# A mixture's first products in a seven-product form, with the tokens taken in three passes

## The chip, the cores and the metric

One core of a Trainium2 chip runs the whole program. The metric is the device time of one execution in microseconds (us). TensorE is PE in the profile, VectorE is DVE, ScalarE is ACT, GpSimd is POOL and SyncE, whose queue starts most transfers, is SP.

## What is computed

Three stages follow one another. A small attention between x (4 batches, 8 heads, 512 positions, 64 wide) and a state of 32 rows gives N = 2176 tokens of 512 (17 tiles of 128 tokens). A first mixture of eight experts is dense: every token goes through every expert, and the weights P come from eight rounds of row and column normalisation over all tokens. A second mixture sends each token to one expert.

```
# first mixture: x (N, 512), w1 (8, 512, 1024), w2 (8, 1024, 512)
logits = x @ w_gate
P = np.exp(logits - logits.max())
for _ in range(8):
    P /= P.sum(1, keepdims=True) + 1e-09
    P /= P.sum(0, keepdims=True) + 1e-09
    P *= N / E
for e in range(E):
    out += P[:, e:e + 1] * (np.maximum(x @ w1[e], 0.0) @ w2[e])
# second mixture
e_idx = np.argmax(out @ w_gate2, axis=1)
h = np.maximum(x[mask] @ w1[e], 0.0)          # mask: tokens of expert e
out[mask] = gate_w[mask, None] * eom[mask, e, None] * (h @ w2[e])
```

## The kernel before

**Operands in two parts.** A product of fp32 operands is made of three matmuls: each operand is split into a high part (a cast on ACT to the matmul's 32-bit format) and a low part (what the cast left over, by a subtraction on another engine), and high·high, high·low and low·high are accumulated in one PSUM bank.

**Start.** The attention of batch 0 (parts c1 to c5 per group of four heads: transposes, scores, softmax, transposes, read) runs before the first product. c5 writes the tokens into `xhi` and `xlo` (L238, L239), which hold all of x, transposed and split, on the chip. The parts of batches 1 to 3 and the other half of the attention (n1 to n3, lagging) are in a queue, and `pump` takes entries from it between groups of matmuls, at a pace set per stage.

**Units.** The first mixture is 32 units: expert × quarter (256 of 1024 hidden columns). `prep` loads 512 KB of w1 and of w2 for one unit, `prep_split` casts on ACT (L367) and subtracts on POOL (L368). Each unit goes over five chunks of tokens, three of 512, one of 384 and one of 256. `mm1` makes the hidden values: two halves of 128 hidden columns, four blocks of K, three matmuls each (L386 to L388), then relu on ACT (L389) and the low part of the hidden values on DVE (L390). `mm2` makes, for each 128-token tile of the chunk before, two blocks × three matmuls of 512 columns (L402 to L404); DVE multiplies by the gate and accumulates (L413).

**Gates.** `gate_a` and `gate_b` make the logits from the split x, with the weights stationary. `sinkhorn` is a chain: `row` on DVE (L328 to L332), `col` a matmul with ones (L337) and four operations on DVE (L338 to L341). They are in the queue too, and done before unit 4. The first expert's outputs are added up without gates until then.

**The last unit and after.** A table, `AFTER`, places in the last unit what follows the first mixture: per tile `final_a` (store, four transposes L430), `final_b` (logits of the second mixture, L441); per group of tiles `route` (ranks among an expert's tokens, L473 to L534, with small matmuls L493); `sel_a` to `sel_c` choose what the second mixture starts with; `split_first` splits the first expert's weights in eight pieces of 1024 (L628: ACT casts, POOL subtracts). The second mixture then goes over 19 slots of 128 tokens (`m1`, `hT`, `m2s`; products L678 to L680 and L703 to L705).

## Time and profile before

| | |
|---|---|
| median of three runs | 1910.68 us (1909.02 to 1911.96) |
| the profiled execution: its span | 1910.8 us; the profile gives no other time for it |
| PE busy | 1859.2 us, 97%, 9073 matmuls |
| DVE, ACT, POOL busy | 828.5, 391.1, 228.4 us |
| from the first product to unit 4 | 29.95 to 300.80 us |
| units 4 to 30 | 300.80 to 1558.10 us |
| last unit | 1558.10 to 1636.00 us |
| second mixture | 1636.00 to 1910.80 us |

A row of the timeline has the start, the length, the engine, the line of the kernel, the operation, out<-in by the program's names and shapes; in brackets the idle time before it and what ended that. Matmuls overlap one another, so the length of one is longer than the distance to the next start; the cost of one in a row of many is that distance. The granted clock is a share of full speed.

### The profile page before, as it was taken

Reading aid. Unit: us, or ns where it says so; the run is one execution under the profiler, and the core shown is the slowest. Engines: PE = TensorE matmul, PEld = TensorE weight load, DVE = VectorE, ACT = ScalarE, POOL = GpSimd, SP = SyncE. Lnnn points to the kernel's source line nnn. Section 1 sums busy time; section 2 is a strip of 40 time slices with the busy share of each in tenths; the row PEclk is TensorE's granted clock in tenths of the full one; section 3 lists DMA queues with packets and bytes.
Section 4 is the critical chain, followed back from the end, with each engine's and each line's share of the span. In section 5 each row is a group of like instructions: output and inputs, shape, how many; then the busy total and the mean of one; then the engine's idle time right before and its main releaser. Section 6 shows DMA issues by size and latency. Waiting matters only on the chain. (4 is left out here: it accounts for less than half of the span.)

```text
span 1910.8 us, 22103 instructions
## 1 busy us (share of the span) xinstructions
PE 1859.2 (97%) x9073; PEld 1572.1 (82%) x9073; DVE 828.5 (43%) x1416; ACT 391.1 (20%) x626; POOL 228.4 (12%) x136
## 2 busy tenths in 40 slices
PE   6999999999999999999999999999999999799998
PEld 5788778888888888888888888888888888678886
DVE  4653565344444434444344344434344435834332
ACT  3332111111111111111111111111111112235332
POOL 2000101111111111111111111111111100422212
PEclk9899999999999999999999999999999999899999
DMA  3110000000000000000000000000000004234121
...
DMA packets 55284, 77.38 MB, mean 40 GB/s; under 512 B 22336, under 2 KB 38720, under 8 KB 52608
## 3 DMA queue, kind: packets, MB, share of 16 engines
...
## 5 line engine op out<-in xcount | busy, mean ns | idle before, releaser
L390 DVE SCALAR_TENSOR_TENSOR hl<-ph,hh 128x512 fp32r<-128x512 f32 (+2 forms) x320 | 195.7, 612 | 608.9 <-ACT hh L389 608.9
L386 PE MATMUL ph<-xhi,wh 128*128 128x512 f32 (+2 forms) x1280 | 459.5, 359 | 0.0
L388 PE MATMUL ph<-xhi,wl 128*128 128x512 f32 (+2 forms) x1280 | 457.3, 357 | 0.0
L387 PE MATMUL ph<-xlo,wh 128*128 128x512 f32 (+2 forms) x1280 | 457.0, 357 | 0.0
L402 PE MATMUL py<-wh,hh 128*128 128x512 f32 x1088 | 428.9, 394 | 0.0
L403 PE MATMUL py<-wl,hh 128*128 128x512 f32 x1088 | 425.8, 391 | 0.0
L404 PE MATMUL py<-wh,hl 128*128 128x512 f32 x1088 | 425.6, 391 | 0.0
L389 ACT ACTIVATE hh<-ph 128x512 fp32r<-128x512 f32 (+2 forms) x320 | 170.9, 534 | 1207.8 <-PE ph L388 1205.2
L413 DVE SCALAR_TENSOR_TENSOR accA<-py,PG,accA 128x512 f32<-128x512 f32 x348 | 261.4, 751 | 168.1 <-PE py L404 165.0
L368 POOL TENSOR_TENSOR wl<-raw,wh 128x1024 fp32r<-128x1024 f32 x64 | 153.2, 2395 | 1372.4 <-ACT wh L367 1372.4
L386 PEld LDWEIGHTS ph<-xhi,wh 128*128 128x128 f32 x1280 | 241.3, 188 | 32.9 <-ACT xhi L238 1.2
L387 PEld LDWEIGHTS ph<-xlo,wh 128*128 128x128 f32 x1280 | 241.3, 189 | 31.7
L388 PEld LDWEIGHTS ph<-xhi,wl 128*128 128x128 f32 x1280 | 241.1, 188 | 30.2
L402 PEld LDWEIGHTS py<-wh,hh 128*128 128x128 f32 x1088 | 205.4, 189 | 45.5 <-issue 5.4
L404 PEld LDWEIGHTS py<-wh,hl 128*128 128x128 f32 x1088 | 205.1, 188 | 43.5
L403 PEld LDWEIGHTS py<-wl,hh 128*128 128x128 f32 x1088 | 205.3, 189 | 39.9
L413 DVE SCALAR_TENSOR_TENSOR accB<-py,PG,accB 128x512 f32<-128x512 f32 x145 | 108.9, 751 | 68.0 <-PE py L404 66.7
L367 ACT CAST wh<-raw 128x1024 fp32r<-128x1024 f32 x64 | 66.7, 1044 | 5.1 <-DMA raw<-in_moe_w_dram 5.1
...
L685 ACT ACTIVATE hs<-pm 128x512 f32<-128x512 f32 x38 | 38.4, 1110 | 30.7 <-PE pm L680 30.7
L695 ACT CAST hh<-pt 128x512 fp32r<-128x512 f32 x38 | 20.4, 590 | 104.1 <-PE pt L692 104.1
L696 DVE TENSOR_TENSOR hl<-pt,hh 128x512 fp32r<-128x512 f32 x38 | 24.4, 685 | 38.5 <-ACT hh L695 38.5
...
## 6 DMA issues: line engine op xcount, KB each, us to landing
raw<-in_moe_w_dram SPq DMA_DIRECT2D x64, 512.0 KB, 3.5
...
xg<-x1d,gi POOLq DMA_INDIRECT x20, 4.6
out_dram<-y,si POOLq DMA_INDIRECT x19, 3.0
```

Of the source, the lines that this page charges most:

```text
L367: nc.scalar.copy(hi, raw)
L368: nc.gpsimd.tensor_tensor(out=lo, in0=raw, in1=hi.bitcast(F32), op=ALU.subtract)
L386: nc.tensor.matmul(ps[:, :n], whi[:, k, f], xhi[:, k, cols], start=(k == 0), stop=False)
L387: nc.tensor.matmul(ps[:, :n], whi[:, k, f], xlo[:, k, cols], start=False, stop=False)
L388: nc.tensor.matmul(ps[:, :n], wlo[:, k, f], xhi[:, k, cols], start=False, stop=(k == KD - 1))
L389: nc.scalar.activation(out=hh[:, ft, :n], in_=ps[:, :n], func=AF.Relu)
L390: nc.vector.scalar_tensor_tensor(out=hl[:, ft, :n], in0=ps[:, :n], scalar=0.0, in1=hh[:, ft, :n].bitcast(F32), op0=ALU.max, op1=ALU.subtract)
L402: nc.tensor.matmul(ps, hh[:, j, r], whi[:, j, :], start=(j == 0), stop=False)
L403: nc.tensor.matmul(ps, hh[:, j, r], wlo[:, j, :], start=False, stop=False)
L404: nc.tensor.matmul(ps, hl[:, j, r], whi[:, j, :], start=False, stop=(j == 1))
L413: nc.vector.scalar_tensor_tensor(out=a, in0=ps, scalar=PG[:, t, e : e + 1], in1=a, op0=ALU.mult, op1=ALU.add)
L685: nc.scalar.activation(out=ov, in_=ps2[n].rearrange("t (p j) -> t p j", j=NJ), func=AF.Relu)
```

## The change

**Three passes.** The tokens are taken in three passes of 768, 768 and 640 (`PASSES`, whose second number is half a pass). A pass goes over all 32 units, so there are 96 steps, and in each step the unit's w1 and w2 are loaded and split. x is no longer kept split: c5 writes the tokens of the first pass into `xst` and those of the other passes to DRAM (`xtd`), from which `xload` brings them back at unit 14 of the pass before.

**Seven products.** w1's unit (512 × 256) and a pass's x (512 × 768) are each cut in 2 × 2 blocks. `mm1` makes seven products of 256 × 128 by 256 × 384 (or 320) in Winograd's form of Strassen's method, in the order 1, 6, 5, 7, 2, 3, 4, where product 2 is accumulated onto product 1 in its bank. It needs four sums of blocks of w1 (`prep_w1`, on POOL, per step; seven operands are then split), four sums of blocks of x (`xsums`, per pass; seven operands, `xsplit`), one copy on ACT and six combinations on DVE (L486 to L506) of the products. The relu (L474) and the low part (L478) follow from the combined blocks; of the four low parts, three now have a block in SBUF as their input, not PSUM.

**What else moves.** Batches 0 and 1 of the attention run before the first product; batches 2 and 3, the lagging parts and the gates are in the queue for steps 0 to 4, the normalisation for steps 5 to 7. The gates are made from unsplit x, tile by tile, with x stationary. In the first pass the first two experts are added up without gates. `final_a` and `final_b` run at the end of each pass, `route` for the first four tiles at step 33, for the next two groups with `sel_a` to `sel_c` at steps 65 to 67. Half of the first expert's pieces are split before the second mixture starts. Buffers of the second mixture are laid into those of the first.

```diff
+    PASSES = [(0, 384), (768, 384), (1536, 320)]
+    HW = 384
...
+    def gate(ts):
         def f():
-            t0, nt = CHUNKS[c]
-            n = nt * P
-            cols = slice(t0 * P, t0 * P + n)
-            ps = bank(f"psg{c}")
-            for k in range(KD):
-                nc.tensor.matmul(ps[:, :n], wg_sp[:, k, :], xhi[:, k, cols], start=(k == 0), stop=False)
-                nc.tensor.matmul(ps[:, :n], wg_sp[:, k, :], xlo[:, k, cols], start=False, stop=(k == KD - 1))
-            lt = ap2.tile([P, 2, S], F32, tag="xT", name=f"lt{c}")[:, 0, :]
-            nc.scalar.copy(lt[0 : 2 * E, :n], ps[0 : 2 * E, :n])
-            lts[c] = lt
+            ps = bank(f"psg{ts[0]}")
+            for i, t in enumerate(ts):
+                for k in range(KD):
+                    if t < 6:
+                        a = XT1[:, k, t * P : (t + 1) * P]
+                    elif t < NT - 1:
+                        a = xtm[t // R, k // 2][:, k % 2, (t % R) * P : (t % R + 1) * P]
+                    else:
+                        a = xs[:, k, :]
+                    nc.tensor.matmul(ps[:, i * E : (i + 1) * E], a, wg[:, k, :], start=(k == 0), stop=(k == KD - 1))
...
+    PROD = {1: (0, 0), 2: (1, 1), 3: (6, 2), 4: (2, 6), 5: (3, 3), 6: (4, 4), 7: (5, 5)}
...
+    def xsums(p, home):
+        b11, b12, b21, b22, w = xquarters(p)
+        t = [home[:, i * XW : i * XW + w].rearrange("p (k n) -> p k n", k=2) for i in range(4)]
+        e = nc.vector if p == 0 else nc.gpsimd
+        return [
+            lambda: e.tensor_tensor(out=t[0], in0=b12, in1=b11, op=ALU.subtract),
+            lambda: e.tensor_tensor(out=t[1], in0=b22, in1=t[0], op=ALU.subtract),
+            lambda: e.tensor_tensor(out=t[2], in0=b22, in1=b12, op=ALU.subtract),
+            lambda: e.tensor_tensor(out=t[3], in0=t[1], in1=b21, op=ALU.subtract),
+        ], t
+    def xsplit(p, t, order=(0, 4, 3, 5, 1, 2, 6), pool=(3, 1, 6)):
+        b11, b12, b21, b22, w = xquarters(p)
+        of = [b11, b21, b22] + t
+        def one(i):
+            def f():
+                hi = xop(i, 0, w).rearrange("p (k n) -> p k n", k=2)
+                lo = xop(i, 1, w).rearrange("p (k n) -> p k n", k=2)
+                nc.scalar.copy(hi, of[i])
+                e = nc.gpsimd if i in pool else nc.vector
+                e.tensor_tensor(out=lo, in0=of[i], in1=hi.bitcast(F32), op=ALU.subtract)
+            return f
+        return [one(i) for i in order]
...
+        def f0():
+            nc.gpsimd.tensor_tensor(out=sv[0], in0=a21, in1=a22, op=ALU.add)
+            nc.gpsimd.tensor_tensor(out=sv[1], in0=sv[0], in1=a11, op=ALU.subtract)
+            nc.gpsimd.tensor_tensor(out=sv[2], in0=a11, in1=a21, op=ALU.subtract)
+            nc.gpsimd.tensor_tensor(out=sv[3], in0=a12, in1=sv[1], op=ALU.subtract)
+            nc.scalar.copy(wop(s, 0, 0, 2).rearrange("p (k f) -> p k f", k=KD), raw[:, :, 0:P])
+            nc.scalar.copy(wop(s, 0, 2, 1).rearrange("p (k f) -> p k f", k=2), a22)
+        def f1():
+            nc.scalar.copy(wop(s, 0, 3, 4), sst.rearrange("p a c -> p (a c)"))
+            r = "p (k f) -> p k f"
+            nc.gpsimd.tensor_tensor(out=wop(s, 1, 0, 2).rearrange(r, k=KD), in0=raw[:, :, 0:P],
+                                    in1=wop(s, 0, 0, 2).rearrange(r, k=KD).bitcast(F32), op=ALU.subtract)
+            nc.gpsimd.tensor_tensor(out=wop(s, 1, 2, 1).rearrange(r, k=2), in0=a22,
+                                    in1=wop(s, 0, 2, 1).rearrange(r, k=2).bitcast(F32), op=ALU.subtract)
+            nc.gpsimd.tensor_tensor(out=wop(s, 1, 3, 4), in0=sst.rearrange("p a c -> p (a c)"),
+                                    in1=wop(s, 0, 3, 4).bitcast(F32), op=ALU.subtract)
...
+        def prod(i, ps, start=True, stop=True):
+            a, b = PROD[i]
+            for k in range(2):
+                wh, wl = (wop(s, lo, a, 1)[:, k * P : (k + 1) * P] for lo in (0, 1))
+                xh, xl = (xop(b, lo, 2 * h)[:, k * h : (k + 1) * h] for lo in (0, 1))
+                nc.tensor.matmul(ps, wh, xh, start=start and k == 0, stop=False, skip_group_check=True)
+                nc.tensor.matmul(ps, wh, xl, start=False, stop=False, skip_group_check=True)
+                nc.tensor.matmul(ps, wl, xh, start=False, stop=stop and k == 1, skip_group_check=True)
...
+        def relu(c, f, half):
+            nc.scalar.activation(out=hh[:, f, half * h : (half + 1) * h], in_=c, func=AF.Relu)
+        def rest(c, f, half):
+            q = slice(half * h, (half + 1) * h)
+            nc.vector.scalar_tensor_tensor(out=hl[:, f, q], in0=c, scalar=0.0, in1=hh[:, f, q].bitcast(F32),
+                                           op0=ALU.max, op1=ALU.subtract)
+        tt = nc.vector.tensor_tensor
+        new(1)
+        nc.scalar.copy(u2, B_[1])
+        between(0)
+        new(6)
+        tt(out=u2, in0=B_[6], in1=u2, op=ALU.add)
+        between(1)
+        new(5)
+        tt(out=u4, in0=B_[5], in1=u2, op=ALU.add)
+        between(2)
+        new(7)
+        tt(out=u3, in0=B_[7], in1=u2, op=ALU.add)
+        between(3)
+        prod(2, B_[1], start=False)
+        tt(out=c22, in0=B_[5], in1=u3, op=ALU.add)
+        relu(B_[1], 0, 0)
+        relu(c22, 1, 1)
+        between(4)
+        new(3)
+        rest(B_[1], 0, 0)
+        tt(out=u4, in0=B_[3], in1=u4, op=ALU.add)
+        relu(u4, 0, 1)
+        rest(c22, 1, 1)
+        between(5)
+        new(4)
+        tt(out=u3, in0=u3, in1=B_[4], op=ALU.subtract)
+        relu(u3, 1, 0)
+        rest(u4, 0, 1)
+        between(6)
+        rest(u3, 1, 0)
...
+        if p == 0 and e < 2:
+            if e == 1:
+                a = xst[:, t * DM : (t + 1) * DM]
+            if q == 0:
+                nc.vector.tensor_copy(a, ps)
+            else:
+                nc.vector.tensor_tensor(out=a, in0=ps, in1=a, op=ALU.add)
+            return
...
+        def step_mm1(s):
+            h = PASSES[s // NU][1]
+            nxt = prep_w1(s + 1) if s < LAST else [lambda: None] * 2
+            def between(i):
+                if i == 1:
+                    prep_w2(s)
+                if i == 3:
+                    nxt[0]()
+                if i == 5:
+                    nxt[1]()
+                pump(PITCH[h])
+            mm1(s, between)
+        def step_mm2(s, hooks={}):
+            for t in tiles_of(s // NU):
+                mm2(s, t)
+                if todo:
+                    todo.pop(0)()
+                pump(1.36)
...
+        queue += [gate(range(0, 4)), gate(range(4, 6)), gate(range(6, 8))]
+        for g in range(G):
+            load_x(2, g)
+        load_state(2)
+        load_state(3)
+        queue += window(2) + window(3)
+        (a0, a1, a2), (b0, b1, b2) = lag[2, 0], lag[2, 1]
+        queue += [a0, b0, a1, b1, seq(a2, lambda: load_x(3, 0)), seq(b2, lambda: load_x(3, 1))]
+        (a0, a1, a2), (b0, b1, b2) = lag[3, 0], lag[3, 1]
+        queue += [a0, b0, a1, b1, a2, b2, seq(gate(range(NT - 1, NT)), states_out)]
+        pace[0] = 66.0 / len(queue)
+        queue += [close_reads] + sinkhorn()
...
+            if p < 2 and u == 14:
+                xload(p + 1)
+            if p < 2 and u == 24:
+                sums, T0 = xsums(p + 1, home[0])
+                queue += sums
+                pace[0] = 4.0
+            if s == NU + 1:
+                queue += list(Rq[0])
+                pace[0] = 3.0
+            if s == 2 * NU + 1:
+                queue += [Rq[1][0], seq(Rq[1][1], sel_a), Rq[1][2], Rq[2][0], sel_b, sel_c, Rq[2][1], load_first, first_rows, Rq[2][2]]
+                pace[0] = 4.0
+            step_mm1(s)
+            if u < NU - 1:
+                if u > 0:
+                    step_mm2(s - 1)
+                continue
+            flush()
+            ts = list(tiles_of(p))
+            if p < 2:
+                todo += xsplit(p + 1, T0)
+                step_mm2(s - 1)
+                hooks = {ts[i]: [A[ts[i - 1]]] + ([Bq[ts[i - 2]]] if i > 1 else []) for i in range(1, 6)}
+                step_mm2(s, hooks)
+                while todo:
+                    todo.pop(0)()
+                queue += [seq(A[ts[5]], Bq[ts[4]]), Bq[ts[5]]]
+                pace[0] = 2.0
+            else:
+                load_first_raw(0, 0)
+                for i in (2, 3, 0, 1):
+                    todo.append(lambda i=i: split_piece(SETS[0], i, 1024, nc.gpsimd))
+                todo.append(lambda: load_first_raw(1, 1))
+                step_mm2(s - 1)
+                step_mm2(s, {13: [A[12]], 14: [A[13], Bq[12]], 15: [A[14], Bq[13]], 16: [Bq[14], A[15], lambda: xT(0)]})
+        for i in range(4, 8):
+            split_piece(SETS[0], i, 1024, nc.gpsimd)
```

On POOL, before, two splits stand per unit (`wl_0` is w1's low part, `wl_1` w2's; a unit has five chunks):

```order
L368 TENSOR_TENSOR wl_1_1707<-raw_1_1622,wh_1_1706 128x1024
L368 TENSOR_TENSOR wl_0_2024<-raw_0_1955,wh_0_2023 128x1024
L368 TENSOR_TENSOR wl_1_2113<-raw_1_2021,wh_1_2112 128x1024
L368 TENSOR_TENSOR wl_0_2366<-raw_0_2311,wh_0_2365 128x1024
L368 TENSOR_TENSOR wl_1_2434<-raw_1_2363,wh_1_2433 128x1024
L368 TENSOR_TENSOR wl_0_2674<-raw_0_2621,wh_0_2673 128x1024
```

Now this stands in each of the 96 steps (`sst` holds the sums of w1's blocks, `XR` the split operands, `rawb` the loaded weights, `wl` is w2's low part):

```order
L443 TENSOR_TENSOR wl_4788<-rawb,wh_4787 128x1024
L418 TENSOR_TENSOR sst<-rawb 128x256
L419 TENSOR_TENSOR sst<-sst,rawb 128x256
L420 TENSOR_TENSOR sst<-rawb 128x256
L421 TENSOR_TENSOR sst<-rawb,sst 128x256
L428 TENSOR_TENSOR XR<-rawb,XR 128x512
L430 TENSOR_TENSOR XR<-rawb,XR 128x256
L432 TENSOR_TENSOR XR<-sst,XR 128x1024
L443 TENSOR_TENSOR wl_4915<-rawb,wh_4914 128x1024
```

So a step has eight operations on POOL where a unit of five chunks had two.

On DVE, this is the middle of step 6, in which a row of the normalisation falls (`p_6` are the banks of the step's products, `u` and `c` the combined blocks, `HB` the hidden values, `PG` the gates):

```order
L495 TENSOR_TENSOR c_106<-p_6_1784,u_104 128x384
L328 TENSOR_REDUCE sm_408<-PG 128x17
L329 TENSOR_SCALAR sm_408<-sm_408 128x17
L330 RECIPROCAL sm_409<-sm_408 128x17
L331 TENSOR_TENSOR PG<-PG,sm_409 128x136
L332 TENSOR_REDUCE sm_410<-PG 128x8
L478 SCALAR_TENSOR_TENSOR HB<-p_6_1757,HB 128x384
L501 TENSOR_TENSOR u_105<-p_6_1820,u_105 128x384
L478 SCALAR_TENSOR_TENSOR HB<-c_106,HB 128x384
L506 TENSOR_TENSOR u_104<-u_104,p_6_1836 128x384
L478 SCALAR_TENSOR_TENSOR HB<-u_105,HB 128x384
L338 TENSOR_SCALAR sm_411<-pscol_1846 128x8
```

The operations L328 to L332, which the column matmul waits for, stand between the step's combinations; L478 with `c` and `u` are the low parts from SBUF.

At the end of the first pass, DVE does the accumulations of the last two steps (`py`, L547) with four splits of the next pass's operands (L392) among them:

```order
L547 SCALAR_TENSOR_TENSOR acc<-py_0_5104,PG,acc 128x512
L392 TENSOR_TENSOR XR<-xst,XR 128x768
L547 SCALAR_TENSOR_TENSOR acc<-py_1_5114,PG,acc 128x512
L392 TENSOR_TENSOR XR<-raw_1582,XR 128x768
L547 SCALAR_TENSOR_TENSOR acc<-py_2_5124,PG,acc 128x512
L547 SCALAR_TENSOR_TENSOR acc<-py_3_5134,PG,acc 128x512
L392 TENSOR_TENSOR XR<-raw_1582,XR 128x768
L547 SCALAR_TENSOR_TENSOR acc<-py_4_5144,PG,acc 128x512
L547 SCALAR_TENSOR_TENSOR acc<-py_5_5154,PG,acc 128x512
L392 TENSOR_TENSOR XR<-xst,XR 128x768
L547 SCALAR_TENSOR_TENSOR acc<-py_0_5164,PG,acc 128x512
L547 SCALAR_TENSOR_TENSOR acc<-py_1_5174,PG,acc 128x512
```

The first transposes of the pass's first tile follow on PE after the matmuls of the second `py` of the last step, and need the accumulation of the first, which is the last row but one; before, no split of x stood on DVE beside the tiles' ends.

## Rows read from the trace of the kernel before

**Rows 1.** The page's first part: busy time, share of the span and instructions of each engine.
```profile
PE 1859.2 (97%) x9073; PEld 1572.1 (82%) x9073; DVE 828.5 (43%) x1416; ACT 391.1 (20%) x626; POOL 228.4 (12%) x136
```

**Rows 2.** Engines by stage: start:end, length, busy us and instructions of each engine, granted clock.
```profile
0.00:29.95 29.95, 16.76 (x66) 12.97 (x66) 11.30 (x21) 7.85 (x12) 3.05 (x7) 1.00 0.53 129
29.95:300.80 270.85, 257.48 (x1360) 215.78 (x1359) 146.05 (x325) 66.51 (x133) 23.49 (x24) 0.97 0.09 26
300.80:1558.10 1257.30, 1257.30 (x5995) 1072.41 (x5994) 512.04 (x731) 194.91 (x324) 129.47 (x54) 1.00 0.07 22
1558.10:1636.00 77.90, 74.02 (x454) 64.53 (x452) 41.01 (x157) 19.89 (x38) 5.32 (x4) 1.00 0.40 142
1636.00:1910.80 274.80, 253.65 (x1202) 206.40 (x1202) 118.14 (x184) 101.92 (x121) 67.06 (x48) 0.96 0.27 99
```

**Rows 3.** Timeline of PE: start, length (us), engine, line; first product of units 4 and 31.
```profile
300.80 0.39 PE L386 MATMUL ph<-xhi,wh 128*128 128x512 f32 x1
...
1558.10 0.39 PE L386 MATMUL ph<-xhi,wh 128*128 128x512 f32 x1
```

**Rows 4.** The same view: starts of a run of 384, 512, 256, 512 columns.
```profile
796.39 0.33 PE L386 MATMUL ph<-xhi,wh 128*128 128x384 f32 x1
...
800.58 0.39 PE L402 MATMUL py<-wh,hh 128*128 128x512 f32 x1
...
806.06 0.28 PE L386 MATMUL ph<-xhi,wh 128*128 128x256 f32 x1
...
808.93 0.40 PE L402 MATMUL py<-wh,hh 128*128 128x512 f32 x1
```

**Rows 5.** Groups by line and shape: count | busy us, mean ns | idle before, releaser.
```profile
L413 DVE SCALAR_TENSOR_TENSOR accA<-py,PG,accA 128x512 f32<-128x512 f32 x348 | 261.4, 751 | 168.1 <-PE py L404 165.0
...
L390 DVE SCALAR_TENSOR_TENSOR hl<-ph,hh 128x384 fp32r<-128x384 f32 x64 | 35.7, 558 | 107.1 <-ACT hh L389 107.1
...
L389 ACT ACTIVATE hh<-ph 128x384 fp32r<-128x384 f32 x64 | 31.5, 492 | 259.0 <-PE ph L388 259.0
...
L367 ACT CAST wh<-raw 128x1024 fp32r<-128x1024 f32 x64 | 66.7, 1044 | 5.1 <-DMA raw<-in_moe_w_dram 5.1
...
L368 POOL TENSOR_TENSOR wl<-raw,wh 128x1024 fp32r<-128x1024 f32 x64 | 153.2, 2395 | 1372.4 <-ACT wh L367 1372.4
```

**Rows 6.** Timeline of all engines beside the start of the second mixture.
```profile
1632.85 18.69 POOL L628 TENSOR_TENSOR xlo<-raw,xhi 128x1024 fp32r<-128x1024 f32 x8
...
1636.85 14.73 DVE L474 TENSOR_TENSOR rt_v<-L,rt_mx 128x24 f32<-128x24 f32 x1
...
1652.27 0.18 PE L493 MATMUL prank<-oh,lowb 128*128 128x24 bf16 x1 [7.69 <-DVE oh L477]
```

**Rows 7.** Timelines of DVE and POOL in the normalisation.
```profile
253.46 2.37 DVE L340 TENSOR_SCALAR sm<-sm 128x8 f32<-128x8 f32 x1
...
253.41 2.39 POOL L368 TENSOR_TENSOR wl<-raw,wh 128x1024 fp32r<-128x1024 f32 x1 [40.87 <-ACT wh L367]
```

**Rows 8.** Engines by stretch, as in rows 2, after two waits of PE.
```profile
53.60:63.60 10.00, 8.94 (x37) 8.28 (x37) 4.69 (x11) 2.81 (x7) 0.00 (x0) 0.50 0.25 56
1647.40:1661.00 13.60, 7.35 (x25) 5.29 (x25) 12.31 (x45) 3.37 (x7) 4.13 (x2) 0.50 0.00 0
...
54.66 0.66 PE L227 MATMUL psa<-ident,e 128*128 128x128 f32 x2 [3.45 <-DVE e L222]
```

**Rows 9.** Timeline of PE: the start, the first unit, and the last unit's gate product.
```profile
11.45 6.93 PE L202 MATMUL pss<-sbd,xT 128*128 128x64 f32 x32
...
45.91 1.90 PE L202 MATMUL pss<-sbd,xT 128*128 128x64 f32 x16
...
1576.68 0.96 PE L441 MATMUL pl<-wr,x1T 128*128 128x16 f32 x8
```

**Rows 10.** DMA issues: queue, operation, count, KB each, median us to landing.
```profile
raw<-in_moe_w_dram SPq DMA_DIRECT2D x64, 512.0 KB, 3.5
```

**Rows 11.** Waits of PE: released by, us in total, times, longest us.
```profile
PE pscol L337 <- DVE sm L332: 4.5, 4, 3.3
```

506 lines of the change are left out of this document (240 added, 266 removed).

## The prediction

> **What bounds the kernel now.** The page's busy shares come first: PE is busy 97% of the span, DVE 43%, POOL 12% [rows 1]. Cut into stages by the engines' view [rows 2], the reader is to see that the middle stage, 27 units long, has 1257.30 us of PE work in 1257.30 us, while the stage in front of it leaves PE idle 13.4 us, the last unit 3.9 and the second mixture 21.2. So in the units every matmul removed is time gained as long as the other engines keep up, and in the three other stages what counts is the waits. A unit lasts (1558.10 − 300.80) / 27 = 46.57 us [rows 3].
>
> **Term 1, the products: −83.** The timeline of PE gives pitches from start to start [rows 4]: 24 matmuls of 384 columns take 4.19 us (0.1746 each), 24 of 256 take 2.87 (0.1196). A unit has 24 of each and 174 of 512 columns (72 in the first products, 102 in the second), so a 512 takes (46.57 − 4.19 − 2.87) / 174 = 0.2271. The new 320 columns lie halfway between 256 and 384: 0.147. A new step has 7 products × 2 K blocks × 3 = 42 short matmuls and 36 (third pass 30) of 512. That is 42 × 0.1746 + 36 × 0.2271 = 15.51 us, and 42 × 0.147 + 30 × 0.2271 = 12.99. Over 32 units: 32 × (2 × 15.51 + 12.99) = 1408 against 32 × 46.57 = 1490. The second products stay as they are; of the first products an eighth goes, which is 5.5% of the unit.
>
> **What a step adds beside PE** is taken as hidden, and this is where the forecast is thinnest. From the groups [rows 5]: ACT gets four relus and one copy at 0.49, casts of 2 × 1.04 and two shorter ones, by their columns about 0.6 and 0.4, together 5.5 us of 15.5. SP moves 512 KB twice per step, each landing in 3.5 us [rows 10]; x through DRAM is loaded once per pass, ten steps ahead. POOL, which split 2 × 1024 columns (2 × 2.395) per 46.57 us, now has per step those two, one split of 512 (1.2), one of 256 (0.6) and four sums of 256 (0.6 each, by the 1024 row divided by four): 9.0 us in one run, queued back to back. It starts once ACT has cast w2, about 2.6 us into the step, and ends at 11.7. DVE has ten operations of 384 columns (0.558) and six accumulations (0.751) where a unit's 46.57 us had ten and seventeen: 10.1 us.
>
> Three of DVE's ten, the remainders of c22, u4 and u3, now read both inputs from SBUF; before, every remainder read PSUM. What such an operation does beside POOL is shown in one place: a tiny comparison, 128x24, lasted 14.73 us, and ended at 1651.58 when POOL's row of eight splits (18.69 us from 1632.85) ended at 1651.54 [rows 6]. So DVE was let in not after POOL's current instruction but after its whole queue. Waits behind a lone split are shorter: 2.37 us for an operation of 128x8 [rows 7]. No DVE operation with a PSUM input is stretched this way.
>
> The Trainium skill, "SBUF — State Buffer", section "Who interferes with whom", says that a DVE instruction with two SBUF inputs contends with a GpSimd instruction that reads SBUF and that whoever issues first holds the shared pair for the whole instruction; by it the wait would end with POOL's current instruction and the waits of terms 2 to 4 would be a few us smaller (rival A). The trace agrees that the two block one another, and not that the lock ends with one instruction.
>
> By the row, the remainder of c22 is issued at about 6.8 us into the step and held to 11.7; then come u3, two remainders and the six accumulations, the last at 18.5, 3.1 us into the next step. DVE's demand is 10.1 + 4.9 = 15.0 of 15.5 us. With eight PSUM banks, the nearest places where PE needs a bank back have 1.5 to 3.6 us in hand, by this count. In the third pass it is ten at 0.49 (an estimate: the 0.558 of the row less an eighth for a sixth fewer columns), five accumulations and a hold of about 4.2: 12.9 of 13.0. I take **0** for both; the ends are 0 and the difference that rival B prices.
>
> **Term 2, the front, to the end of the normalisation: +23.**
> - Forward part of the second batch before the first product: the first batch's takes 29.95 us with 16.76 us of PE in it [rows 2]; the second fills part of the 13.2 us of idle: +11 (ends 5 and 17). It leaves the queue beside the first units: −8, half of the 16.76, since warm transposes and matmuls there take about half (16 calls of 64 columns 1.90 us, when the first 32 took 6.93) [rows 9].
> - The first operands: after the last of x, two sums and two splits on DVE (768 columns, a little under twice the 0.558 of 384, 1.0 each) before the second product: +4.
> - The gate matmuls are now 17 tiles at four fp32 matmuls with x stationary. The nearest row has the same form with 16 columns, 0.96 us for one tile (its four fp32 matmuls are recorded as eight) [rows 9]; I take 0.9 for eight columns, 15 us for all. Before it was 8 matmuls per chunk at the pitches above (7.8) and 17 small ones at a quarter of 0.96 (4.1): +3 (ends −4 and +4).
> - The lock. In steps 5 to 7 the column sums wait for a chain of five small DVE operations, and the four places of such a chain in a step lie under POOL's 9 us run for more than half. Before, the same waits cost 4.5 us in four places [rows 11]. I take 13: four waits of 2 to 3 us, and half of a clock fall (below); ends 3 and 24.
>
> **Clock.** After PE waits of 3.45 and 7.69 us the granted clock was 0.50 for 10.0 and 13.6 us, which had 8.94 and 7.35 us of matmuls in them [rows 6, 8]; at the full level (2.4 GHz, against 1.2) they would have taken half: 3.5 to 4.5 us per fall.
>
> **Term 3, two changes of pass: +18.** The first transposes of a finished tile wait for its accumulation, which is behind DVE's lag, four splits of x operands and the hold: ready at about 24.3 us of the last step, asked for at 18.2. That is 6 us, and a clock fall of 3 after it, twice. Ends 8 and 28.
>
> **Term 4, the routes: +18.** Ranks, counts and tables for the first eleven tiles are moved from the last unit, where they lay beside 512-column work, into steps 33 and 65 to 67: chains of some ten small SBUF operations with PE waiting for their result, under POOL's run half of the time. Three waits of 3 to 4 us, two clock falls at 3.5, and 1 us of matmuls; ends 6 and 32. The operations themselves are the same.
>
> **Term 5, the end: −5.** Half of the first expert's eight splits is done before the second mixture, so POOL's row beside its first block is about 9.4 us, not 18.7, and the wait of 7.69 with its clock fall [rows 6, 8] shrinks. Ends −11 and 0.
>
> **Sum:** −83 + 23 + 18 + 18 − 5 = −29, on the profiled execution's span of 1910.8, which is 0.1 above the median of the runs: **1882**. With the ends not all on one side, 1850 to 1910.
>
> **Rivals.**
> - *A, the port is handed over after each POOL instruction* (faster). Then no wait is over 2.4 us: the lock in term 2 is 3, terms 3 and 4 about 6 each, −83 + 13 + 6 + 6 − 5 = −63: **1848**. For it: the waits behind lone splits; against it: the 14.73 us. Chance 0.23.
> - *B, DVE becomes the bound* (slower). The hold does not shrink as DVE falls behind, or POOL's run ends later than 11.7 because its last split waits for ACT's cast; the accumulations come late and PE waits for a bank in every step. At 1 us per step that is 96 on top: 1882 + 96 = **1978**. It decides from 29 / 96 = 0.3 us per step on, so a hold of 5.7 instead of 4.9 us is enough. For it: 15.0 of 15.5 and 12.9 of 13.0. Against it: the hold is a time on POOL's clock and is shorter the later DVE arrives. Chance 0.2.
> - *C, shorter matmuls do not pay*: if 384 columns cost what 512 do, 64 × 42 × 0.0525 = 141 more, and no gain. The 256 and 384 rows [rows 4] speak against it: chance 0.02.
>
> **How the numbers follow.** The forecast has 0.55. About 4 us (0.2%) is what a measurement here can tell. The forecast's own range holds little above 1907: 0.04 for no change and 0.03 for slower. With A faster and B and C slower, B's weak form (0.3 us and less per step) counted as faster: faster 0.74, same 0.04, slower 0.22. For 8 in 10 the range goes from below A's value (its smallest seams, 1828) to a B of half a us per step: 1882 + 48 = 1930.
>
> **What would show it.** Right: steps of 15.5 and 13.0 us with PE without idle, a remainder of c22 lasting about 5 us and ending with POOL's run; the three seams with PE waits of 3 to 7 us and a clock of 0.5 after them. Rival A: that remainder lasts under 2.4 us. Wrong: PE idle in each step, released by an accumulation or a combination on DVE; or a pitch of 384 columns other than 0.175.

## The result and the profile after

The changed kernel takes 1880.78 us (median of 4 runs, 1877.62 to 1882.32), the kernel before 1911.22 beside it: a ratio of 0.9845, 95% interval 0.9829 to 0.9862. The forecast was 1882. The profiled execution took 1879.49 us, its span is 1877.8; against the span of before that is 33.0 us less, and the rows below are held against that.

The first part of the page of the kernel after, to be read with [rows 1]: DVE has gone from 43% to 65% and POOL from 12% to 59%, and PE is still the engine that is full.

```profile
PE 1804.5 (96%) x9327; PEld 1607.7 (86%) x9327; DVE 1211.8 (65%) x2041; ACT 653.3 (35%) x1114; POOL 1099.3 (59%) x857
```

Engines by stage of the kernel after (columns as in [rows 2]; the last two numbers of a row are the mean busy share of the DMA engines and the GB/s that they moved): the front up to the end of the normalisation in three rows, the steps that merge the first experts' sums, 20 steps of the first pass, 29 of the second, the second mixture.

```profile
0.00:40.54 40.54, 29.22 (x132) 23.70 (x133) 18.58 (x38) 15.77 (x29) 7.82 (x13) 0.87 0.42 97
40.54:192.43 151.89, 143.07 (x814) 128.80 (x815) 92.86 (x167) 51.98 (x107) 54.82 (x43) 0.88 0.36 96
192.43:261.67 69.24, 58.01 (x253) 49.19 (x252) 55.49 (x123) 16.08 (x28) 29.38 (x24) 0.88 0.15 46
261.67:312.50 50.83, 47.34 (x235) 42.01 (x234) 39.54 (x55) 15.47 (x27) 33.73 (x39) 1.00 0.21 62
312.50:622.65 310.15, 310.15 (x1561) 281.23 (x1560) 210.54 (x326) 103.12 (x180) 217.29 (x165) 1.00 0.24 74
692.00:1141.60 449.60, 449.60 (x2263) 407.70 (x2262) 302.14 (x469) 149.63 (x261) 310.56 (x236) 1.00 0.23 71
...
1617.70:1877.80 260.10, 245.06 (x1202) 203.28 (x1202) 111.92 (x184) 101.49 (x120) 59.55 (x45) 0.98 0.30 104
```

In the long stretches PE has no idle time, 310.15 us in 310.15, so a step is 310.15 / 20 = 15.51 us, and in the third pass it is 12.98. The loss is at the ends of these stretches: the rows of the front have a clock of 0.87 and 0.88 where before they had 1.00 and 0.97 [rows 2], and in the 69.24 us of the normalisation PE stands for 11.2, and the mean clock is 0.88.

The waits of PE after (columns as in [rows 11]) name the places:

```profile
PE pscol L337 <- DVE sm L332: 11.2, 6, 3.7
PE prank L628 <- DVE oh L612: 9.9, 3, 4.1
PE pf L565 <- DVE acc L547: 6.7, 2, 4.0
...
PE pgat L681 <- DVE osg L739: 4.6, 1, 4.6
```

Now the middle of one step, DVE and then POOL, in the timeline after. `HB<-c` and `HB<-u` are the low parts with two SBUF inputs.

```profile
551.13 0.56 DVE L478 SCALAR_TENSOR_TENSOR HB<-p,HB 128x384 fp32r<-128x384 f32 x1 [0.47 <-ACT HB L474]
551.60 0.55 DVE L501 TENSOR_TENSOR u<-p,u 128x384 f32<-128x384 f32 x1
552.07 0.85 DVE L478 SCALAR_TENSOR_TENSOR HB<-c,HB 128x384 fp32r<-128x384 f32 x1
552.84 0.54 DVE L506 TENSOR_TENSOR u<-u,p 128x384 f32<-128x384 f32 x1
553.30 0.63 DVE L478 SCALAR_TENSOR_TENSOR HB<-u,HB 128x384 fp32r<-128x384 f32 x1
555.05 1.14 DVE L478 SCALAR_TENSOR_TENSOR HB<-u,HB 128x384 fp32r<-128x384 f32 x1 [1.13 <-ACT HB L474]
```

```profile
551.75 0.74 POOL L420 TENSOR_TENSOR sst<-rawb 128x256 f32<-128x256 f32 x1
552.45 1.06 POOL L421 TENSOR_TENSOR sst<-rawb,sst 128x256 f32<-128x256 f32 x1
553.47 1.61 POOL L428 TENSOR_TENSOR XR<-rawb,XR 128x512 fp32r<-128x512 f32 x1
555.04 0.74 POOL L430 TENSOR_TENSOR XR<-rawb,XR 128x256 fp32r<-128x256 f32 x1
555.74 2.73 POOL L432 TENSOR_TENSOR XR<-sst,XR 128x1024 fp32r<-128x1024 f32 x1
```

The first low part from SBUF takes 0.85 us, not 5: it gets in when L420 ends, POOL's next instruction is lengthened by it (1.06 for 0.74), and so on in turn. POOL's queue is full from 547.9 to 558.5, yet DVE does not wait here for more than the instruction that is running. The rule of the Trainium skill, "SBUF — State Buffer", section "Who interferes with whom", that the first to issue holds the shared pair for the whole instruction, agrees with these rows; the forecast's longer hold does not.

### The profile page after: what moved, and what is told of

It reads as the page before. It is cut to its first block, busy times and chain, and to the rows that moved or that the text cites. A ratio compares the mean times of both kernels' runs of the same rounds, so it can differ in the third digit from the quotient of the medians.

```text
span 1877.8 us, 25502 instructions
## 1 busy us (share of the span) xinstructions
PE 1804.5 (96%) x9327; PEld 1607.7 (86%) x9327; DVE 1211.8 (65%) x2041; ACT 653.3 (35%) x1114; POOL 1099.3 (59%) x857
## 4 chain that ended last, share of the span: by engine, by line
PE 74%; DVE 9%; issue 9%; DMA 5%; POOL 2%; ACT 1%; SPq 0%; POOLq 0%; DVEq 0%; ACTq 0%
PE py L527 12%; PE py L528 12%; PE py L529 12%; PE p L465 11%; PE p L467 11%; PE p L466 11%; DMA out_dram<-xst,si 4%; DMA out_dram<-y,si 1%; DVE HB L478 1%; PE psg L303 1%; PE psr L281 1%; PE pss L206 1%; PE pl L576 1%; DVE acc L547 1%; PE pso L243 1%
## 5 line engine op out<-in xcount | busy, mean ns | idle before, releaser
L443 POOL TENSOR_TENSOR wl<-rawb,wh 128x1024 fp32r<-128x1024 f32 x96 | 230.8, 2405 | 473.1 <-ACT wh L442 473.1
L465 PE MATMUL p<-XR 128*128 128x384 f32 (+1 forms) x1344 | 447.9, 333 | 4.2 <-ACT XR L390 2.8
L467 PE MATMUL p<-XR 128*128 128x384 f32 (+1 forms) x1344 | 444.1, 330 | 4.1 <-POOL XR L432 3.0
L466 PE MATMUL p<-XR 128*128 128x384 f32 (+1 forms) x1344 | 443.7, 330 | 0.9 <-DVE XR L392 0.9
L527 PE MATMUL py<-wh,HB 128*128 128x512 f32 x1088 | 431.6, 397 | 2.4 <-DVE acc L547 2.3
L528 PE MATMUL py<-wl,HB 128*128 128x512 f32 x1088 | 429.0, 394 | 0.0
L529 PE MATMUL py<-wh,HB 128*128 128x512 f32 x1088 | 428.6, 394 | 0.0
L547 DVE SCALAR_TENSOR_TENSOR acc<-py,PG,acc 128x512 f32<-128x512 f32 x485 | 338.9, 741 | 79.3 <-PE py L529 78.7
L432 POOL TENSOR_TENSOR XR<-sst,XR 128x1024 fp32r<-128x1024 f32 x96 | 255.0, 2656 | 50.8 <-ACT XR L426 50.8
L465 PEld LDWEIGHTS p<-XR 128*128 128x128 f32 x1344 | 256.8, 191 | 11.3 <-ACT XR L390 4.1
L467 PEld LDWEIGHTS p<-XR 128*128 128x128 f32 x1344 | 256.5, 191 | 5.4 <-POOL XR L432 3.8
L466 PEld LDWEIGHTS p<-XR 128*128 128x128 f32 x1344 | 256.7, 191 | 4.9 <-DVE XR L392 1.5
L478 DVE SCALAR_TENSOR_TENSOR HB<-u,HB 128x384 fp32r<-128x384 f32 (+1 forms) x192 | 169.3, 883 | 117.4 <-ACT HB L474 117.2
L529 PEld LDWEIGHTS py<-wh,HB 128*128 128x128 f32 x1088 | 206.7, 190 | 44.2
L527 PEld LDWEIGHTS py<-wh,HB 128*128 128x128 f32 x1088 | 206.8, 190 | 44.0 <-DVE acc L547 3.0
L528 PEld LDWEIGHTS py<-wl,HB 128*128 128x128 f32 x1088 | 206.6, 190 | 39.7
L474 ACT ACTIVATE HB<-u 128x384 fp32r<-128x384 f32 (+1 forms) x192 | 96.9, 505 | 80.0 <-DVE u L501 72.2
L486 DVE TENSOR_TENSOR u<-p,u 128x384 f32<-128x384 f32 (+1 forms) x96 | 51.3, 534 | 112.6 <-PE p L467 108.2
L474 ACT ACTIVATE HB<-p 128x384 fp32r<-128x384 f32 (+1 forms) x96 | 45.5, 474 | 190.4 <-PE p L467 190.4
```

What stands on the lines that cost most here:

```text
L432: nc.gpsimd.tensor_tensor(out=wop(s, 1, 3, 4), in0=sst.rearrange("p a c -> p (a c)"), in1=wop(s, 0, 3, 4).bitcast(F32), op=ALU.subtract)
L443: nc.gpsimd.tensor_tensor(out=lo, in0=raw, in1=hi.bitcast(F32), op=ALU.subtract)
L465: nc.tensor.matmul(ps, wh, xh, start=start and k == 0, stop=False, skip_group_check=True)
L466: nc.tensor.matmul(ps, wh, xl, start=False, stop=False, skip_group_check=True)
L467: nc.tensor.matmul(ps, wl, xh, start=False, stop=stop and k == 1, skip_group_check=True)
L474: nc.scalar.activation(out=hh[:, f, half * h : (half + 1) * h], in_=c, func=AF.Relu)
```

## The experiments

To read the runs, each stage's length is taken from the first products of its steps, less its steps at their undisturbed length (15.51 and 12.98 us with seven products, 16.55 and 13.86 with eight) and less the other matmuls of `mm1` and `mm2` that fall in it. What is left is what the stage costs on top, in us (the stages at the change of pass contain the tiles' own transposes and logits; the last column runs from the last step's matmuls to the end):

| kernel | start | steps 0–4 | 5–7 | 8–10 | 31–32 | 33–36 | 63–64 | 65–70 | 71–94 | end |
|---|---|---|---|---|---|---|---|---|---|---|
| after | 40.5 | 82.5 | 22.7 | 4.3 | 15.6 | 7.1 | 11.1 | 20.1 | 0.0 | 265.9 |
| eight | 41.2 | 73.2 | 7.7 | 0.0 | 8.1 | 1.5 | 8.2 | 3.9 | 0.0 | 270.0 |
| eight_pool | 41.3 | 68.4 | 9.9 | 0.0 | 8.5 | 7.1 | 8.2 | 14.4 | 0.0 | 269.2 |
| pool_more | 44.6 | 88.3 | 30.7 | 8.5 | 15.1 | 9.8 | 13.5 | 32.0 | 16.6 | 266.7 |
| gates_first | 42.2 | 74.7 | 22.6 | 4.3 | 15.6 | 7.1 | 11.1 | 20.1 | 0.0 | 265.8 |
| late_routes | 40.8 | 84.3 | 21.6 | 4.9 | 16.7 | 4.4 | 11.1 | 13.8 | 0.6 | 266.6 |
| psum_rest | 42.7 | 71.1 | 13.9 | 4.2 | 11.4 | 4.1 | 10.2 | 8.7 | 0.6 | 266.6 |

One stage of the same code differs by up to 4 us between two executions (63–64 was 11.1 to 15.5 over the runs that leave it alone), so only larger differences are read.

**Eight products, same passes (eight).** The seven products are undone, the passes kept (`half` is one block product, two K blocks × three matmuls):

```diff
-        new(1)
-        nc.scalar.copy(u2, B_[1])
...
-        rest(u3, 1, 0)
+        for i in range(2):
+            for c in range(2):
+                ps = bank(f"p{i}{c}_{s}")[:, :h]
+                for j in range(2):
+                    half(i, c, j, ps)
+                    if j == 1:
+                        relu(ps, i, c)
+                        rest(ps, i, c)
```

> Eight plain block products in place of seven, the same three passes, no sums of blocks, no combinations; the result is the same. Theory 1 (the products are bound by PE alone, the rest of a step is hidden in either form): a step has 48 short matmuls, 48 x 0.1746 + 36 x 0.2271 = 16.56 us in the first two passes and 48 x 0.147 + 30 x 0.2271 = 13.87 in the third, so 32 x (2 x 1.05 + 0.89) = 96 us more than with seven, less some 5 us at the start, where no sums of x are awaited: about 1970. Theory 2 (the sums on POOL and the combinations on DVE make a good part of the waits between the stages): 15 us or more are given back between the stages, 1960 or less, with waits at the column sums well under the 11 us of the changed kernel.

1914.36 us, 1.0031 of before (1.0019 to 1.0043). The steps are 16.55 and 13.86 us as both theories had it, 95 us more than with seven; but the medians are 34 us apart, not 95. By the table the stages between give back 60: 15 in the normalisation, 9 in steps 0 to 4, 16 in steps 65 to 70, and the rest in smaller parts. The waits say the same:

```profile
PE prank L597 <- DVE oh L581: 4.8, 3, 2.4
PE pscol L337 <- DVE sm L332: 4.4, 4, 2.0
```

So the passes, with all that was moved for them, cost 0.3%; the seven products gain 95 us in the steps and lose some 60 of them between the stages. Theory 2 held. What it leaves open is whether POOL's sums or DVE's combinations do it.

**POOL's longest instruction twice (pool_more).** One line repeated, the low part of the four sums:

```diff
+            nc.gpsimd.tensor_tensor(out=wop(s, 1, 3, 4), in0=sst.rearrange("p a c -> p (a c)"),
+                                    in1=wop(s, 0, 3, 4).bitcast(F32), op=ALU.subtract)
```

> The changed kernel with POOL's last and longest low part of w1 (1024 columns) made twice in every step. Theory 2 (DVE's operations with two SBUF inputs are held until POOL's whole queue is through, as the prediction took it): the hold is some 2.5 us longer, DVE goes over the step, about 2 us per step in the first two passes and more in the third, 150 to 220 us in all: 2030 to 2100. Theory 1 (the port is handed over after each POOL instruction): the steps of the first two passes stay at 15.5 us; only where POOL itself is full, in the third pass (10.3 of 13.0 us busy, then 12.9), a step may grow by up to 0.5 us: 1878 to 1897.

1939.84 us in one run. The steps of passes one and two stay at 15.51 us (4.5 us more over 46 of them), which ends the hold through the whole queue: with it each would have grown by 2. But theory 1's time is missed by 40 us too: the third pass grows by 0.7 us a step (16.6 in steps 71 to 94, where POOL is busy 304.62 of 328.08 us), and the normalisation by 8 us, steps 65 to 70 by 12; most other stages with a chain grow by 2 to 6, which one execution hardly tells from noise, and steps 31 to 32 don't. So POOL's length matters where PE waits for a chain on DVE, and in the third pass, where PE waits for POOL itself.

```profile
PE p L469 <- POOL XR L434: 27.5, 20, 4.0
PE pscol L337 <- DVE sm L332: 18.8, 7, 5.2
PE prank L630 <- DVE oh L614: 13.6, 3, 6.0
```

**POOL's work without the combinations (eight_pool).** To the eight-product kernel POOL's four sums and a low part of 768 columns are added, so that POOL has the columns of the seven-product form again; the results are not used.

```diff
+            nc.gpsimd.tensor_tensor(out=sv[0], in0=a21, in1=a22, op=ALU.add)
...
+            nc.gpsimd.tensor_tensor(out=wop(s, 1, 4, 3), in0=sst.rearrange("p a c -> p (a c)")[:, 0:768],
+                                    in1=wop(s, 0, 4, 3).bitcast(F32), op=ALU.subtract)
```

> The kernel with eight products, with POOL's work of the seven-product form put back (four sums of 256, low parts of 1024 + 768 instead of 1024; results unused), but without the combinations on DVE and with every low part of the hidden values from PSUM. Theory 1 (POOL's instructions on the shared port make the waits between the stages): these come back, steps 5 to 7 take 65 us or more (57.4 with eight products alone, of which 49.7 are matmuls), and the whole goes from 1914 to 1940 to 1960. Theory 2 (DVE's longer queue makes them): the whole stays under 1925, steps 5 to 7 under 60.

1930.72 us, 1.0106 of before (1.0090 to 1.0121): between the two. Most of the routes' cost comes back (33–36 from 1.5 to 7.1, 65–70 from 3.9 to 14.4 of 20.1), the normalisation's doesn't (9.9 against 22.7). For the routes POOL's work alone brings most of it; in the normalisation it takes POOL and what the combinations bring, which is work on DVE and three low parts that read SBUF.

**POOL quiet in the normalisation (quiet_norm).** In `prep_w1` for steps 6 to 8, f0 (likewise) and f1 keep only their casts:

```diff
         def f1():
+            if 6 <= s <= 8:
+                nc.scalar.copy(wop(s, 0, 3, 4), sst.rearrange("p a c -> p (a c)"))
+                load_raw(s + 1, 0)
+                return
```

> The changed kernel, but POOL's sums and low parts of w1 are left out for steps 6 to 8, so that POOL has only w2's low part during steps 5 to 7, where the normalisation runs (those three units are computed with stale operands). In the changed kernel these three steps take 23.5 + 21.6 + 24.1 = 69.2 us, where the matmuls alone take 46.5, and the column sums wait 11.2 us. Theory 1 (the small DVE operations of a round are each blocked by one POOL instruction): the waits fall to under 5 us, the clock does not fall, the three steps take 50 to 58 us. Theory 2 (DVE's own queue, its ten operations per step, is what the round stands behind): the waits stay at 9 us or more, the three steps at 64 to 69.

Theory 1's numbers came: steps 5 to 7 take 53.9 us, not 69.2, the clock stays at 1.00, and the column sums wait 3.1 us. Which operations of DVE POOL held is left open by it. (The whole, 1877.38, can't be compared: with other values other experts are chosen, and the second mixture is another.)

```profile
197.00:250.86 53.86, 50.66 (x254) 43.76 (x253) 45.54 (x123) 15.97 (x28) 7.22 (x3) 1.00 0.17 59
```

```profile
PE pscol L337 <- DVE sm L332: 3.1, 6, 1.2
```

**The chain's own operations out of POOL's way (psum_norm).** The reciprocals and factors of the normalisation go to PSUM, so that none of its multiplications has two SBUF inputs.

```diff
-            nc.vector.reciprocal(rr, rs)
+            rp = bank("psrow")[:, 0:NT]
+            nc.vector.reciprocal(rp, rs)
...
+                cr = ps[:, 64 : 64 + E]
```

> The changed kernel with the reciprocals of the row sums and the column factors of the normalisation kept in PSUM banks, so that no multiplication of the chain has two SBUF inputs and none of its scalings both ends in SBUF; POOL's work is unchanged. Theory 1 (each such operation waits for one POOL instruction, and that is what the column sums wait for): as with POOL quiet there, though the step's own three low parts still wait: pscol waits of 4 to 6 us, steps 5 to 7 at 55 to 62 us in place of 69, 7 to 14 us gained: 1867 to 1874. Theory 2 (the gain with POOL quiet came from the step's own operations on DVE being free, not from the chain's): under 4 us gained, waits of 9 us or more.

1880.42 us, 0.9854 of before (0.9835 to 0.9872), which is the changed kernel's ratio. Theory 1 as it was put fell, and theory 2's signs came: the chain's operations now take 0.2 to 0.4 us each, and still the column sums wait 9.6 us. DVE's timeline of this run shows what they stand behind: two low parts of the step's own, 3.54 us for what is 1.1, ahead of the factors that the next row needs.

```profile
202.33 3.54 DVE L480 SCALAR_TENSOR_TENSOR HB<-u,HB 128x384 fp32r<-128x384 f32 x2
205.79 0.68 DVE L538 COPY xst<-py 128x512 f32<-128x512 f32 x1
206.39 0.16 DVE L340 TENSOR_SCALAR pscol<-pscol 128x8 f32<-128x8 f32 x1
```

Not only operations with two SBUF inputs were held. The scaling of the column factors has one input; from SBUF to SBUF it took 0.67 us in the mean and up to 2.30 in the kernel after (first row), and in PSUM it takes 0.17 every time (second row, this run).

```profile
L340 DVE TENSOR_SCALAR sm<-sm 128x8 f32<-128x8 f32 x8 | 5.4, 670 | 0.3
L342 DVE TENSOR_SCALAR pscol<-pscol 128x8 f32<-128x8 f32 x8 | 1.4, 174 | 0.3
```

**The routes' small tiles in PSUM (psum_routes).**

```diff
+            pt = bank(f"prt{c}")
+            mx, mr = pt[:, 0:n], pt[:, 8 : 8 + n]
+            v = pt[:, 64 : 64 + n * E].rearrange("p (t e) -> p t e", e=E)
```

> The changed kernel with the small tiles of the routes (maxima, masks, ranks, factors) in a PSUM bank, the spacing as it is. Theory 1 (the routes' waits are POOL's instructions, one per operation with two SBUF inputs): the waits for prank fall from 9.9 to about 4 us, steps 33 and 65 to 66 lose 4 to 9 us with their clock falls, and the row of small operations at the start of the second mixture 3 to 5: 8 to 14 us gained, 1867 to 1873. Theory 2 (with the eight-product kernel it was the step being emptier): under 4 us gained.

1878.56 us, ratio 0.9832 (0.9815 to 0.9848): some 2 us at most. The waits for prank fall to 5.6, and steps 33 to 36 cost 7.3, as in the kernel after. Theory 1 missed here too; a gain under 4 us is what theory 2 had.

**The spacing of the routes (late_routes).**

```diff
-                pace[0] = 3.0
+                pace[0] = 10.0
...
-                pace[0] = 4.0
+                pace[0] = 9.0
```

> The changed kernel with the pieces of the routes and of the choice for the second mixture spaced 9 to 10 us apart in the queue, not 3 to 4. Theory 1 (PE waits there because a matmul of a chain is issued before DVE has come to its end; with 9 us between them the end is there): the waits for prank and pgat in steps 33 and 65 to 66 (4.1, 3.4 and 4.6 us) and the clock falls behind them go, 12 to 18 us gained: 1863 to 1869. Theory 2 (these operations are held by POOL's queue for up to 9 us wherever they are put): some of the waits stay, under 6 us gained.

1872.08 us, ratio 0.9799 (0.9780 to 0.9819), 9 us, between theory 1's 12 to 18 and theory 2's 6. Steps 33 to 36 and 65 to 70 lose 2.7 and 6.3 us. PE now waits more for POOL's low part of w1, 6.9 us in place of 3.0:

```profile
PE p L467 <- POOL XR L432: 6.9, 5, 2.4
```

Of these, 2.1 us fall in step 33 and 4.0 in the third pass, where the kernel after has 2.4; the expectation of late_w1 puts all 6.9 in the third pass. What makes them longer is not shown: in steps 65 to 70 this instruction of POOL lasts 2.44 us in the mean, against 2.53 in the kernel after.

**The gates ahead of the first products (gates_first).** `gate` for tiles 0 to 3 is emitted before the first product, for 4 to 7 behind it.

```diff
         C1[4]()
+        g0[0]()
...
+                if s == 0 and i == 0:
+                    g1[0]()
+                    g2[0]()
```

> The changed kernel with the gate matmuls of the first eight tiles moved to where PE waits for the first operands: four tiles ahead of the first product, four behind it. Theory 1 (a wait of PE costs itself and a stretch at half clock behind it: after the waits of 1.5 and 1.4 us at 39 and 43 us the clock is at 0.50 to about 69 us): PE has work there, the stretch at half clock gets much shorter, 8 to 16 us are gained: 1865 to 1873. Theory 2 (the clock there does not hang on these waits): only the idle time is filled, 2 to 4 us: 1877 to 1879.

1873.16 us, ratio 0.9810 (0.9793 to 0.9828): 7 us, at the edge of theory 1 and outside theory 2. The gain is one of the clock. After, in windows (as [rows 8]), then with the gates first:

```profile
40.00:48.00 8.00, 5.26 (x18) 4.09 (x18) 6.50 (x6) 2.23 (x4) 1.85 (x1) 0.64 0.77 197
48.00:56.00 8.00, 8.00 (x36) 8.00 (x36) 4.85 (x5) 2.94 (x4) 3.66 (x2) 0.50 0.04 8
56.00:64.00 8.00, 8.00 (x38) 8.00 (x36) 1.95 (x5) 2.25 (x4) 5.42 (x6) 0.50 0.25 76
64.00:72.00 8.00, 8.00 (x37) 7.87 (x38) 4.15 (x10) 3.24 (x6) 2.44 (x3) 0.66 0.22 67
```

```profile
40.00:48.00 8.00, 8.00 (x49) 8.00 (x48) 6.23 (x5) 2.24 (x4) 1.84 (x1) 0.68 0.77 195
48.00:56.00 8.00, 4.74 (x19) 4.23 (x18) 4.86 (x5) 2.57 (x4) 3.66 (x2) 0.50 0.05 10
56.00:64.00 8.00, 7.86 (x42) 7.73 (x43) 4.08 (x13) 4.00 (x8) 5.80 (x6) 0.76 0.35 87
64.00:72.00 8.00, 6.75 (x49) 6.39 (x47) 6.96 (x16) 4.04 (x8) 4.17 (x3) 1.00 0.82 186
```

The clock (0.50 is the lower level, 1.2 GHz) is back about 10 us earlier: of the 32 us some 17 are at the lower level and not 27, by the four means. But the clock falls without the first waits too. With them filled PE is busy without a gap from 38.62 us on, and still the clock falls at 42.80; PE then stands 3.40 us for the load of a later batch's state:

```profile
38.62:42.80 4.18, 4.18 (x37) 4.18 (x36) 3.79 (x7) 1.38 (x3) 0.00 (x0) 1.00 0.55 164
42.80:52.70 9.90, 9.90 (x43) 9.43 (x41) 8.01 (x7) 4.70 (x6) 3.71 (x3) 0.50 0.40 90
...
56.14 0.66 PE L166 MATMUL psst<-ident,stp 128*128 128x128 f32 x2 [3.40 <-DMA stp<-in_state_dram]
```

So theory 1's time came nearly, and its reason did not. Why the stretch at the lower level is shorter here is open.

**Order on POOL (late_w1, best1).** `prep_w1` of the next step ahead of `prep_w2`, with the late routes, and in best1 with the gates first too.

```diff
-                if i == 1:
-                    prep_w2(s)
-                if i == 3:
+                if i == 0:
                     nxt[0]()
-                if i == 5:
+                if i == 3:
                     nxt[1]()
+                if i == 5:
+                    prep_w2(s)
```

> The kernel with the late routes, and in every step w1's sums and low parts for the next step ahead of w2's low part, not behind it. With the late routes PE waits 6.9 us for POOL's low part of w1 in the third pass, since POOL is busy for 10.3 of 13.0 us and what DVE takes of the port comes on top. Theory 1 (it is the order on POOL: w1 is wanted 5 us before w2): these waits go, steps 67 to 70 come to within 0.3 us of 12.98, 5 to 10 us gained against 1872: 1862 to 1867. Theory 2 (POOL is full there whatever the order): the same time is waited for w2's low part: 1869 to 1875.

> Late routes, w1 ahead of w2 on POOL, and the gate matmuls in the first waits, together. If the three places are independent their gains add: 1881 less 9 (routes), 7 (gates) and 5 to 10 (order): 1855 to 1861. If they are not (a wait filled at one place only moves to the next one): 1865 or more.

1880.71 us (1871.15 to 1882.90 in five runs) and 1861.57 (1855.43 to 1868.00), ratios 0.9839 and 0.9750. The first is as slow as the kernel after and outside both theories, the second half a us above the range for gains that add. The waits for POOL's low part of w1 are no longer among PE's longest, but steps 34 and 35 are 1.5 us longer each, and the runs spread over 12 us where the others spread over 3 to 6 (the profiled execution is the fastest in both); what that is stays open. The order gained nothing that shows; against late_routes the median is some 8 us longer.

**The low parts out of POOL's way (psum_rest).** The last combination of each block is written into its product's bank, with the gates first and the late routes:

```diff
-        tt(out=c22, in0=B_[5], in1=u3, op=ALU.add)
+        tt(out=B_[5], in0=B_[5], in1=u3, op=ALU.add)
+        c22 = B_[5]
```

(u4 into the bank of product 3 and u3 into that of product 4 likewise.)

> The changed kernel with three edits: the last combination of each of the three hidden blocks is written back into the PSUM bank of its product, so that all four low parts read PSUM; the gate matmuls in the first waits and the late routes as before. The first edit is read from the steps that the other two do not touch. Theory 1 (the chain of the normalisation stands on DVE behind the step's own low parts, and those wait for POOL's instructions): the low parts take 0.56 us each, POOL's 1024-column low part 2.4 in place of 2.66 us, the column sums wait 6 us or less, steps 5 to 7 take 56 to 62 us in place of 69; in the third pass POOL has room again and the waits of the late routes for it (6.9 us) go. With 7 and 9 us of the other two: 1850 to 1858. Theory 2 (the chain's length itself and the clock make these waits): steps 5 to 7 stay at 66 us or more, and the whole comes to 1863 to 1867.

1844.57 us, ratio 0.9673 (0.9655 to 0.9690), the fastest of all and better than expected. The groups show that the low parts and POOL's long instruction are no longer lengthened; after, and then in this run:

```profile
L478 DVE SCALAR_TENSOR_TENSOR HB<-u,HB 128x384 fp32r<-128x384 f32 x128 | 119.0, 931 | 61.7 <-ACT HB L474 61.5
L478 DVE SCALAR_TENSOR_TENSOR HB<-c,HB 128x384 fp32r<-128x384 f32 x64 | 52.5, 821 | 0.0
...
L432 POOL TENSOR_TENSOR XR<-sst,XR 128x1024 fp32r<-128x1024 f32 x96 | 255.0, 2656 | 50.8 <-ACT XR L426 50.8
```

```profile
L487 DVE SCALAR_TENSOR_TENSOR HB<-p,HB 128x384 fp32r<-128x384 f32 x256 | 141.6, 553 | 86.2 <-ACT HB L483 86.0
...
L441 POOL TENSOR_TENSOR XR<-sst,XR 128x1024 fp32r<-128x1024 f32 x96 | 230.2, 2398 | 36.1 <-ACT XR L435 35.9 <-PE py L541 0.2
```

Steps 5 to 7, which the other two edits don't touch (69.1 and 68.1 us with one of them alone), take 60.4 us in place of 69.2, with the clock at 0.97, not 0.88:

```profile
183.16:243.58 60.42, 52.07 (x253) 44.88 (x252) 50.99 (x123) 15.77 (x28) 28.84 (x24) 0.97 0.17 53
```

The column sums still wait 8.3 us (six or less was expected), in smaller pieces, and PE waits 4.8 us for POOL's low part of w1, where these waits were to go. Together with quiet_norm and psum_norm this shows the larger part of the mechanism: a chain of the normalisation stands in DVE's queue behind the step's low parts, and these wait for POOL's instructions. On top of their matmuls steps 5 to 7 cost 22.7 us after, 13.9 here and 7.3 with POOL quiet, so the low parts are some 9 of POOL's 15 us; the rest is not taken apart. The clock went with PE's waits: 0.88 with 11.2 us of them, 0.97 with 8.3, 1.00 with 3.1.

**The kernel before, once more, with no edit (before_again).**

> The kernel before, once more, for one row of its trace: the small comparison on DVE that lasted 14.73 us and ended with POOL's row of eight splits. In none of the runs of the other kernels was an operation of DVE stretched over more than about one of POOL's instructions. Theory 1 (handing over after each POOL instruction is the rule, and that row an exception of one execution): it lasts 2.4 us or less here. Theory 2 (it is a property of this place of the kernel before): 12 us or more again.

The row of [rows 6] is there again: 14.40 us, to the end of POOL's eight splits.

```profile
1629.48 14.40 DVE L474 TENSOR_TENSOR rt_v<-L,rt_mx 128x24 f32<-128x24 f32 x1
```

```profile
1625.18 18.66 POOL L628 TENSOR_TENSOR xlo<-raw,xhi 128x1024 fp32r<-128x1024 f32 x8
```

So it belongs to that place. In the changed kernel the same operations stand beside four of the same splits and are let in after each:

```profile
1618.77 2.35 DVE L610 TENSOR_TENSOR rt_v<-rt_v,rev 128x24 f32<-128x24 f32 x1
1621.36 2.07 DVE L612 TENSOR_TENSOR oh<-rev,rt_mr 128x24 bf16<-128x24 f32 x1
1623.36 2.42 DVE L613 TENSOR_TENSOR rt_d<-L,rt_mx 128x24 f32<-128x24 f32 x1
...
1618.67 9.38 POOL L773 TENSOR_TENSOR XR<-raw,XR 128x1024 fp32r<-128x1024 f32 x4 [8.69 <-ACT XR L772]
```

What makes the difference is not known; no run changed one thing at that place.

## Why the prediction was right

The sign and the steps were right by the working. That the whole came within 2 us (4 in the spans) was in part luck: the mechanism behind terms 2 to 4, DVE held through POOL's whole queue, did not occur, the costs came to about their sizes by another path, and what the front and steps 8 to 10 cost more (5.5 and 4.3 us) was given back by terms 3 to 5 (4.9 and 9.7). Rival A, which had the hold right, was 33 us off.

- **Term 1**, −83: the steps are 15.51 and 12.98 us, as worked out from the pitches to 0.01 us; 1408 against 1490 us, −82.
- **Beside PE**: taken as hidden, and it was: no idle time of PE in the undisturbed steps. The reason given was wrong. "DVE was let in not after POOL's current instruction but after its whole queue" is the step that failed: the remainder of c22 took 0.82 us in the mean, not 5, and DVE is busy 67% of a step in the second pass (302.14 of 449.60), not 97%. Rival A had the mechanism. That also makes B, chance 0.2, far less likely than it seemed: pool_more, with 2.4 us more on POOL, left the steps of passes one and two nearly alone; in the third pass, where POOL was then full, a step did grow by 0.7 us. POOL's own run was sized too small: 10.7 us a step (310.56 / 29), where 9.0 were counted, since a sum of 256 columns takes 0.74 to 0.98 us and not 0.6, and the low parts are lengthened.
- **Term 2**, +23 within 0 to 41: the first product is at 40.54 us (some 41 forecast), and the front as a whole is 28.5 us longer: 40.5 + 82.5 + 22.7 against 29.95 and the 87.3 us that the first four units had on top (270.85 less 4 × 46.57, and 2.7 of matmuls left to the next unit). It was put down to a lock of the chain's own operations; quiet_norm shows that POOL's work is worth 15 us in steps 5 to 7, psum_norm and psum_rest that most of this goes by way of the low parts queued ahead, and gates_first gains some 7 us at the start with a shorter stretch at the lower clock, a cost that the prediction did not count there. A term was left out: 4.3 us in steps 8 to 10, where the sums of two experts are merged and PE waits for `acc` three times.
- **Terms 3 and 4**, +36: changes of pass and routes cost 26.7 + 27.2 us and the tiles' ends in the last pass 5.8, where the last unit of before had 28.6 us of all this (77.90 − 46.57 − 2.7): +31. The places are those forecast, and the waits for the ranks are too (4.1 and 3.4 us); those for the first transposes are 4.0 and 2.7 us, where 6 was forecast for each.
- **Term 5**, −5 within −11 and 0: the second mixture takes 260.1 us in place of 274.8, −14.7, outside the ends. The wait of 7.69 us for the ranks [rows 6] fell to 2.49, and the clock there rose from 0.96 [rows 2] to 0.98; with the same 1202 matmuls PE stands 15.0 us in place of 21.2 and is busy 245.06 in place of 253.65. The forecast had only halved the row of splits; that DVE is let in between them here is seen in the rows above, but no run tells its share.
- **Sum:** −82.2 + 28.5 + 4.3 + 31.1 − 14.7 = −33.0, the difference of the spans, where the forecast had −29.
- **Rival A** named 1848 for the right mechanism. Its price was the step that failed: one wait of at most 2.4 us per place. A place has several such operations in a row, and others queued behind them (the ranks' chain at the start of the second mixture was held three times, 2.35, 2.07 and 2.42 us), and PE's waits were up to 4.6 us: the eight-product kernel, with less on both engines, is 60 us cheaper between the steps.
